# Gate products one product pair later, and three weight-sum stores one group later, in a gated SSM and MLP mixer

## The chip, the cores and the metric

The kernel runs on one core of a Trainium2 chip. The metric is the device time of one execution in microseconds (us). Three runs of the kernel before gave 563.6, 562.41 and 564.23 us; their median is 563.6 us.

## The reference

With x of 2048 tokens by 1024 features in bfloat16:

```python
g = sigmoid((x * gate_w).sum(-1))              # one gate per token
Bu = x @ B_bar.T                               # complex, 1024 states
h[t] = Lam_bar * h[t-1] + Bu[t]                # recurrence over 2048 tokens
a = 2 * Re(h @ C.T) + x * Dskip
b = gelu(layernorm(x) @ w1 + b1) @ w2 + b2     # F = 3584
out = g * a + (1 - g) * b
```

## The kernel before

**Products.** Nearly all matrix products are made by a scheme with seven products in place of eight: a 2 by 2 block product is cut into products p1 to p7 of blocks and of sums of blocks (class SG, L830 to L882; all of them go through `mm`, L813, whose first matmul stands on L822 or L824). The sums are made by VectorE through `dve_tt` (L885). The order on TensorE inside one group is p1, p7 of the group before, p5, p6, p2, p3, p4 of the group before.

**Stages on TensorE.** First x and B are transposed (L650, L666) and B's product with x is formed ("Bu"): `bu_plain(pt, c)` (L905) makes the plain product of state tile pt with token chunk c, one 8-matmul product each for the real and the imaginary part; it is used for pt 0 and 1 with chunks 0 and 1, and all else of Bu goes by `bu_group`. `z_gate(pr)` (L1027) makes the gate's sums over features for the two chunks of half pr: 16 matmuls with a two-column stationary matrix (L1036) into PSUM bank 7, then two evictions by ScalarE (L1043). Bank 7 is also one of the two banks (7 and 3) that the transposes of x and B go through; `t_b` (L657) evicts them on ScalarE (L670). Chunk 1 of x comes transposed by a DMA (L980).

Then comes the MLP: blocks "m" (x @ w1, seven groups each, `m_group`, L1254) and "b" (h @ w2, four groups, `b_group`) for two halves of F and two halves of the tokens, and at last the groups "y" (h @ C). The first block "m" is called here by its groups m0 to m6. The recurrence (`ssm`, L1123) is done by VectorE at a low priority between all this.

**W1.** Four slots (W1R, 7168 bytes per partition each) hold w1 column tiles and their sums. `w1_prep` (L1212) loads a tile (L1220), makes four sums in place (`dve_tt`), and, where the tile is wanted again in the second block, stores tile and sums to DRAM with a DMA from GpSimd's queue (L1235, 128 times 7168 bytes). The first four tiles are prepared ahead of the first block; of these the first three are stored, from slots 0, 1 and 2, and are loaded again (L1217) in the second block. The tile of m4 goes to slot 0, that of m5 to slot 1, that of m6 to slot 2: each load waits for the last product that reads the slot, and for the store from it. W2 comes in quarters (`w2_step`, L1285, load L1292, sums by `dve_tt`), one at the end of each of m0 to m3.

**Order.** `build` writes down a graph of tasks; `Graph.add` finds what each depends on, and a planner (`_schedule_once`, L225) simulates it with fixed costs and priorities and so fixes, before the run, the order of the instructions of every engine and queue. TensorE's order is fixed already: every product depends on the one before (`pe_last`). Each engine, and SyncE's and GpSimd's DMA queues, take their instructions in that order and wait at each. A change of the graph may change the planned order anywhere behind it on VectorE, ScalarE and both queues.

Of the kernel before, what the change touches and what calls it, by code (L numbers as in the profile page):

```python
# [419 lines left out]
def build(nc, A_x, A_Lambda_re, A_Lambda_im, A_B_re, A_B_im, A_C_re, A_C_im, A_log_dt, A_Dskip,  # L420
# [23 lines left out]
    g = Graph()  # L444
    es = ExitStack()
    with es:
# [73 lines left out]
        def ssem(name, k, final=False):  # L520
            key = (name, k)
            if key not in slot_sems:
                slot_sems[key] = sem("d_%s%d" % (name, k), dram=final)
                if final:
                    final_sems.append(slot_sems[key])
            return slot_sems[key]
# [378 lines left out]
        def bu_plain(pt, c):  # L905

            if c % 2 == 0:
                cev[pt, c // 2] = nxt("ev", NEV)
            ks = cev[pt, c // 2]
            for ri in range(2):  # L910
                bk = (4, 5, 6, 0, 1, 2)[nxt("cbank", 6)]
                ws = [AR.v(bqo(pt, 2 * ri) + dt * 256, [(1, 128)]) for dt in range(DT)]
                q = mm("bu%d.%d.%d" % (pt, c, ri), bk, ws, [xt(dt, c) for dt in range(DT)], True)
                ev = u_ev(pt, c // 2, ks, ri, c % 2)
                g.add("act", c_act(CH), (1.0, q), lambda e, ev=ev, bk=bk: e.activation(ev.ap, V(PS[bk], 0, [(1, 2 * T)]), AF.Copy),  # L915
                      reads=[b_ps[bk]], writes=[ev, b_ps[bk]], name="u%d.%d.%d" % (pt, c, ri))
                if c % 2 == 1:
                    u_store(pt, c // 2, ks, q, ri)
# [108 lines left out]
        def z_gate(pr):  # L1027

            cs = (2 * pr, 2 * pr + 1)
            xs = [[xt(dt, c) for c in cs] for dt in range(DT)]  # L1030

            def em(e):
                ins = None
                for dt in range(DT):
                    for i, c in enumerate(cs):
                        ins = e.matmul(bass.AP(PS[7], 32 * c * 512, [[512, 2], [1, CH]]), V(GWC, 2 * dt, [(1, 2)]), xs[dt][i].ap, start=(dt == 0), stop=(dt == DT - 1))  # L1036
                return ins
            seq[0] += 1
            t = g.add("pe", 1.0, (1.0, seq[0]), em, reads=xs + [b_gwc], writes=[b_ps[7]], name="z%d" % pr, extra=pe_last)
            pe_last[:] = [t]  # L1040
            for c in cs:
                o = bass.AP(AR.h[F32], 32 * c * zrow + ZR // 4, [[zrow, 2], [1, CH]])
                g.add("act", c_act(CH), (1.0, seq[0]), lambda e, c=c, o=o: e.activation(o, bass.AP(PS[7], 32 * c * 512, [[512, 2], [1, CH]]), AF.Copy),  # L1043
                      reads=[b_ps[7]], writes=[zr, b_ps[7]], name="ze%d" % c)
# [24 lines left out]
        for k in range(4, NTT):  # L1069
            load_x(k, (0.5, k))  # L1070
        for c in range(2):
            if c == 1:
                z_gate(0)
            for pt in range(2):
                bu_plain(pt, c)
        x_sums(0, seq[0])
        order = [(2, 0), (3, 0), (0, 1), (1, 1), (2, 1), (3, 1)] + [(pt, pr) for pt in range(4, PT) for pr in range(2)]
        summed = set()
# [133 lines left out]
        def w1_prep(j, first, q, o0, keep):  # L1212
            s = (o0 - W1R) // 7168
            w1slot[j] = o0
            if not first:
                o = AR.v(o0, [(1, 3584)])
                g.dma((10.0, q - 7), lambda e: e.dma_start(out=o.ap, in_=W1S[j]), 128 * 7168, ssem("w1", s), reads=[b_w1s[j]], writes=[o], name="w1l%d" % j)  # L1217
                return
            o = AR.v(o0, [(256, DT), (1, 256)])
            g.dma((10.0, q - 7), lambda e: e.dma_start(out=o.ap, in_=B_w1[:, j * 256:(j + 1) * 256].rearrange("(dt p) f -> p dt f", p=128)),  # L1220
                  D * 256 * 2, ssem("w1", s), writes=[o], name="w1_%d" % j, bw=DMA_BW_512)

            def raw(fo, dh, dt=BF16):
                return AR.v(o0 + (dh * 1024 + fo * 128) * 2, [(256, 4), (1, 128)], dt)

            def sq(i):
                return AR.v(o0 + 4096 + i * 1024, [(128, 4), (1, 128)], FP16)
            dve_tt("w1a%d" % j, q, sq(0), raw(1, 0), raw(1, 1), ALU.add, 512)
            dve_tt("w1b%d" % j, q, sq(1), sq(0), raw(0, 0), ALU.subtract, 512)
            dve_tt("w1c%d" % j, q, sq(2), raw(0, 0), raw(1, 0), ALU.subtract, 512)  # L1230
            dve_tt("w1d%d" % j, q, raw(1, 0, FP16), raw(0, 1), sq(1), ALU.subtract, 512)
            if not keep:
                return
            ov = AR.v(o0, [(1, 3584)])
            g.dma((10.0, q), lambda e: e.dma_start(out=W1S[j], in_=ov.ap), 128 * 7168, ssem("w1s", s, True), reads=[ov], writes=[b_w1s[j]], name="w1s%d" % j, q="pool")  # L1235

        def w1_st(j):
            o0 = w1slot[j]
# [265 lines left out]
        for n, it in enumerate(flat):  # L1504
            bi, x = it
            kind, Fh, c = blocks[bi]
            last_of_block = (n + 1 == len(flat)) or flat[n + 1][0] != bi
            nit = None if n + 1 == len(flat) else flat[n + 1]
            if (kind, Fh, c, x) == ("b", 1, 0, 3):
                y_load(0)  # L1510
                y_load(1)
            if (kind, x) == ("y", 0):
                y_load(2)
            if cur is None:
                cur = make(it)
                cur.p1()

            if prev is not None:
                prev.p7()
            if kind == "b" and x + 1 < 4:  # L1520
                prep_s((bi, x + 1), seq[0] + 4)
            if kind == "b" and Fh == 1 and c == 0 and x == 3:
                y_prep(0, seq[0] + 4)
            if kind == "y":
                if x + 1 < 8:
                    y_prep(x + 1, seq[0] + 4)
            if not early5:
                cur.p5()
            early5 = False
            cur.p6()  # L1530
            cur.p2()
            if nit is None:
                cur.p7()
            cur.p3()
            if prev is not None:
                prev.p4()
                if kind == "y" and 1 <= x and x + 2 < 8:
                    y_load(x + 2)
                if kind == "m":
                    w2_step(seq[0] + 19)  # L1540
                if kind == "m" and x > 0:
                    w1_next(18)
            if n == 0:
                def em_b2(e):
                    return [e.dma_start(out=v.ap, in_=bass.AP(B_b2.tensor, B_b2.offset + o, [[0, 128], [1, 512]])) for (v, o) in ((v_b2l, 0), (v_b2r, 512))]
                g.dma((40.0, 0), em_b2, 128 * 2048, sem("d_b2b"), writes=[v_b2l, v_b2r], name="b2b", ndma=2)
                g.add("dve", c_dve(512), (40.0, 1), lambda e: e.tensor_tensor(v_b2d.ap, v_b2r.ap, v_b2l.ap, ALU.subtract), reads=[v_b2l, v_b2r], writes=[v_b2d], name="b2d")
                for pg in range(PG):
                    for q in range(NQ):
                        ssm(pg, q)  # L1550
            prev, cur = cur, pend
            pend = None
            if last_of_block:
                if nit is None:
                    prev.p4()
                else:
                    nk = blocks[nit[0]][0]
                    if nk == "b":
                        prep = True
                        b0 = None  # L1560

                        cur = make(nit)
                        prev.p7()
                        cur.p1()
                        prev.p4()
                        w1_next(20)
                        prep_s(nit, seq[0])
                        pend = make((nit[0], nit[1] + 1))
                        pend.p1()
                    else:  # L1570
                        cur = make(nit)
                        prev.p7()
                        cur.p1()
                        cur.p5()
                        early5 = True
                        prev.p4()
                    prev = None
                if (kind, Fh, c) == ("m", 1, 0):
                    ct_load(seq[0] + 20)

                if kind == "m":
                    if (Fh, c) == (0, 0):
                        xn_load(1, seq[0] + 20)
                    elif (Fh, c) == (1, 1):
                        xn_load(0, seq[0] + 20)
                elif (Fh, c) == (0, 1):
                    w2_load(1)
# [43 lines left out]
```

## Time and profile before

| | |
|---|---|
| median of three runs | 563.6 us |
| the profiled execution | 563.84 us, its span 562.1 us |
| TensorE (PE) busy | 545.5 us, 97% of the span |
| VectorE (DVE) busy | 511.8 us, 91% |
| ScalarE (ACT) busy | 288.1 us, 51% |
| GpSimd (POOL) busy | 91.3 us, 16% |
| DMA | 120.08 MB, mean 214 GB/s |

A busy time is the time in which an engine had an instruction running. The chain that ended last goes through TensorE for 80% of the span and through VectorE for 14%. The times of the rows below count from the start of the span; a number in brackets at a row's end is how long the engine sat idle before it and what ended that. Behind a DMA the last number is the time from its issue until it had landed. The DMA share is the busy share of the 16 DMA engines; it can come out a little over 1.

### The profile page before, as it was taken

To read this page: it belongs to the slowest core of one execution; us is meant where nothing else is said; L and a number is where in the kernel's file an instruction comes from. 1 tells how busy PE (TensorE), PEld (TensorE's weight loads), DVE (VectorE), ACT (ScalarE), POOL (GpSimd) and SP (SyncE) were. 2 spreads that over 40 slices of the span, in tenths; PEclk is the share of its full clock that TensorE was granted. 3 is DMA by queue.
4 is the path that set the end of the run, shared out by engine and by line. 5 is a ranking of instruction groups with operands and counts; after the bars stand their busy time and mean duration, and the time that the engine had idled before them with its cause. 6 is when DMAs were issued, how large, how long until landed. Compare 5 with 4: busy or idle time off the path is not lost.

```text
span 562.1 us, 7384 instructions
## 1 busy us (share of the span) xinstructions
PE 545.5 (97%) x2553; PEld 249.2 (44%) x2601; DVE 511.8 (91%) x866; ACT 288.1 (51%) x481; POOL 91.3 (16%) x146
## 2 busy tenths in 40 slices
PE   5899999999999999999999999999999999999997
PEld 4444444444444444444444444444444444444443
DVE  3889899999999999999999999999999886978873
ACT  2978989667774247774246663236663322111110
POOL 0023757630000110011110000211000211001000
DMA  9994999989672444565456957688479999686621
GB/s 271 233 303 96 268 239 311 338 267 350 203 176 100 169 157 180 204 198 224 183 191 200 294 126 149 146 165 240 169 187 189 279 313 293 231 324 224 194 106 56
DMA packets 114911, 120.08 MB, mean 214 GB/s; under 512 B 70322, under 2 KB 92594, under 8 KB 113850
## 3 DMA queue, kind: packets, MB, share of 16 engines
q1 hardware_dynamic: 102256, 73.69, 47.0%
q0 software_dynamic: 12480, 45.90, 26.8%
q8 instruction: 20, 0.33, 0.2%
q14 instruction: 17, 0.14, 0.1%
q10 hardware_dynamic: 138, 0.02, 0.0%
HBM read 56.40 MB, written 47.46 MB: 185 GB/s over the span
## 4 chain that ended last, share of the span: by engine, by line
PE 80%; DVE 14%; issue 3%; ACT 2%; DMA 1%; SPq 0%; DVEq 0%; ACTq 0%
PE ps L824 59%; PE ps L822 19%; DVE ar L885 5%; DVE ar L1269 3%; DVE ar L1145 2%; DVE ar L1159 2%; DVE ar L1148 1%; DMA ar<-in_A_x_dram 1%; ACT ar L670 1%; PE ps L1036 1%; PE ps L650 0%; DVE ar L1352 0%; ACT ar L915 0%; ACT L714 0%; DVE ar L966 0%
## 5 line engine op out<-in xcount | busy, mean ns | idle before, releaser
L824 PE MATMUL ps<-ar 128*128 128x512 f16 (+1 forms) x1792 | 411.8, 379 | 4.7 <-DVE ar L1269 0.8
L824 PEld LDWEIGHTS ps<-ar 128*128 128x128 f16 (+1 forms) x1832 | 178.3, 98 | 221.0 <-ACT ps L857 2.8
L822 PE MATMUL ps<-ar 128*128 128x512 bf16 (+1 forms) x632 | 155.5, 379 | 1.3 <-DVE ar L885 0.9
L885 DVE TENSOR_TENSOR ar<-ar 128x512 f16<-128x512 bf16 (+6 forms) x216 | 139.1, 686 | 6.2 <-PE ps L822 1.8
L822 PEld LDWEIGHTS ps<-ar 128*128 128x128 bf16 (+1 forms) x640 | 61.9, 98 | 76.7 <-DVE ar L885 2.2
L1159 DVE TENSOR_TENSOR_SCAN ar<-cst,init,ar 128x256 bf16<-128x256 f32 x128 | 87.9, 735 | 0.4
L841 ACT ACTIVATE ar<-ps 128x512 f32<-128x512 f32 x100 | 59.0, 593 | 48.3 <-PE ps L822 37.8
L1145 DVE TENSOR_TENSOR ar<-ar 128x2048 bf16<-128x2048 bf16 x64 | 77.0, 1219 | 0.0
L857 ACT ACTIVATE ps<-ps 128x512 f32<-128x512 f32 x66 | 38.5, 583 | 69.9 <-PE ps L822 64.9
L1265 ACT ACTIVATE ar<-ps,cst 128x512 bf16<-128x512 f32 x56 | 38.4, 686 | 19.2 <-PE ps L824 18.5
L842 ACT ACTIVATE ar<-ps,cst 128x512 f32<-128x512 f32 x32 | 22.0, 688 | 49.2 <-PE ps L824 26.0
L1271 ACT ACTIVATE ar<-ar,cst 128x512 bf16<-128x512 f32 x56 | 40.1, 716 | 8.0 <-DVE ar L1269 7.7
L1349 ACT ACTIVATE ar<-ps,cst 128x512 f32<-128x512 f32 x32 | 22.0, 688 | 40.9 <-PE ps L824 40.6
L1148 DVE TENSOR_TENSOR ar<-ar 128x1024 bf16<-128x1024 bf16 x64 | 42.2, 686 | 0.1
L1269 DVE TENSOR_TENSOR ar<-ps,ar 128x512 f32<-128x512 f32 x56 | 38.4, 685 | 3.1 <-PE ps L824 2.5
L900 POOL DMA_DIRECT2D scr_u<-ar x32 | 25.1, 787 | 63.8 <-ACT ar L915 28.9
L1450 DVE SCALAR_TENSOR_TENSOR ar<-ps,cst,ar 128x512 bf16<-128x512 f32 x32 | 23.8, 749 | 12.1 <-PE ps L824 11.9
L1177 POOL DMA_DIRECT2D scr_h<-ar x16 | 9.6, 601 | 123.1 <-DVE ar L1148 123.1
L1352 DVE SCALAR_TENSOR_TENSOR ar<-ps,cst,ar 128x512 f32<-128x512 f32 x32 | 23.8, 744 | 4.4 <-PE ps L824 4.1
L1361 POOL DMA_DIRECT2D scr_ac<-ar x16 | 13.8, 879 | 83.5 <-DVE ar L1352 31.6
L1429 DVE SCALAR_TENSOR_TENSOR ar<-ar,cst 128x1024 f32<-128x1024 bf16 x16 | 20.4, 1282 | 0.2
L1359 POOL DMA_DIRECT2D scr_ac<-ar x16 | 8.5, 534 | 70.7 <-DVE ar L1352 41.0
(104 smaller groups left out, 244.2 us busy)
## 6 DMA issues: line engine op xcount, KB each, us to landing
scr_ac<-ar POOLq DMA_DIRECT2D x32, 512.0 KB, 5.0
ar<-in_A_x_dram SPq DMA_DIRECT2D x32, 256.0 KB, 5.2
scr_u<-ar POOLq DMA_DIRECT2D x32, 256.0 KB, 5.8
ar<-scr_u SPq DMA_DIRECT2D x16, 512.0 KB, 5.0
scr_h<-ar POOLq DMA_DIRECT2D x16, 512.0 KB, 5.8
ar<-scr_ac SPq DMA_DIRECT2D x16, 512.0 KB, 6.6
ar<-scr_h SPq DMA_DIRECT2D x8, 1024.0 KB, 7.3
ar<-in_B_w_dram SPq DMA_DIRECT2D x14, 512.0 KB, 6.8
```

Of the source, the lines that this page charges most:

```text
L822: ins = e.matmul(V(PS[bk], 0, [(1, n)]), st[i].ap, mv[i].ap, start=(i == 0), stop=(i == K - 1))
L824: ins = e.matmul(V(PS[bk], 0, [(1, n)]), st[i].ap, mv[i].ap, start=False, stop=(i == K - 1), skip_group_check=True)
L841: return e.activation(o.ap, V(PS[bk], 0, [(1, 512)]), AF.Copy)
L857: g.add("act", c_act(512), (pb[0], q - 2), lambda e: e.activation(V(PS[b], 0, [(1, 512)]), V(PS[a], 0, [(1, 512)]), AF.Copy), reads=[b_ps[ ...
L885: g.add("dve", c_tt16(n), (pb[0], q), lambda e: e.tensor_tensor(o.ap, a.ap, b.ap, op), reads=[a, b], writes=[o], name=nm).slack = slack
L900: g.dma((1.0, q), lambda e: e.dma_start(out=US[pt // 4, :, 4 * pr:4 * pr + 4, r0:r0 + T], in_=evv.ap), 2 * 128 * CH * 2, ssem("us", 2 * ks ...
L1145: g.add("dve", c_tt16(UE), pri(i), lambda e: e.tensor_tensor(o.ap, a.ap, tbl.ap, ALU.mult), reads=[a, tbl], writes=[o], name=nm + tag)
L1148: g.add("dve", c_tt16(UE // 2), pri(i), lambda e: e.tensor_tensor(o.ap, a.ap, b.ap, op), reads=[a, b], writes=[o], name=nm + tag)
L1159: lambda e, pt=pt, ri=ri, vin=vin, go=go: e.tensor_tensor_scan(go.ap, Cb("R", pt, T), vin.ap, V(INIT, pt * 2 + ri, [(1, 1)]), ALU.mult, AL ...
L1265: g.add("act", c_act(512, ap_operands=1), (10.0, q + 1), lambda e: e.activation(o.ap, V(PS[bk], 0, [(1, 512)]), AF.Gelu_apprx_tanh, bias=C ...
L1269: g.add("dve", c_dve(512), (10.0, q - 2), lambda e: e.tensor_tensor(sv.ap, V(PS[bk], 0, [(1, 512)]), sv.ap, ALU.add), reads=[b_ps[bk], sv] ...
L1271: g.add("act", c_act(512, psum=False, ap_operands=1), (10.0, q + 3), lambda e: e.activation(o.ap, sv.ap, AF.Gelu_apprx_tanh, bias=C("B1", ...
```

## The change

Two things. `z_gate(0)` is called after `bu_plain(0, 1)` instead of before it. And the stores of w1 tiles that are prepared ahead of the first block (those made while no product has been put down since the end of Bu) are not put down at once: their numbers are kept in a list, and the stores are put down at the start of the second round of the loop over groups (n == 1), with a dependence on the last product put down by then, which is p4 of the last Bu group, at the end of m0's products.

```diff
         for c in range(2):
-            if c == 1:
-                z_gate(0)
             for pt in range(2):
                 bu_plain(pt, c)
+                if (c, pt) == (1, 0):
+                    z_gate(0)
         x_sums(0, seq[0])
...
             if not keep:
                 return
+            if seq[0] == bu_seq[0]:
+                w1_held.append(j)
+            else:
+                w1_store(j)
+
+        w1_held = []
+        bu_seq = [seq[0]]
+
+        def w1_store(j, extra=()):
+            o0 = w1slot[j]
+            q = seq[0]
             ov = AR.v(o0, [(1, 3584)])
-            g.dma((10.0, q), lambda e: e.dma_start(out=W1S[j], in_=ov.ap), 128 * 7168, ssem("w1s", s, True), reads=[ov], writes=[b_w1s[j]], name="w1s%d" % j, q="pool")
+            g.dma((10.0, q), lambda e: e.dma_start(out=W1S[j], in_=ov.ap), 128 * 7168, ssem("w1s", (o0 - W1R) // 7168, True), reads=[ov], writes=[b_w1s[j]], name="w1s%d" % j, q="pool", extra=extra)
...
                 y_load(2)
+            if n == 1:
+                for j in w1_held:
+                    w1_store(j, pe_last)
             if cur is None:
                 cur = make(it)
                 cur.p1()
```

## Rows read from the trace of the kernel before

**Rows 1.** The page, engines: busy us, share of the span, instructions.
```profile
PE 545.5 (97%) x2553; PEld 249.2 (44%) x2601; DVE 511.8 (91%) x866; ACT 288.1 (51%) x481; POOL 91.3 (16%) x146
```
**Rows 2.** Waits of PE from 23 us on: total us, times, longest.
```profile
PE ps L1036 <- DVE ar L762: 1.4, 1, 1.4
PE ps L822 <- DVE ar L885: 0.9, 1, 0.9
PE ps L824 <- DVE ar L1269: 0.8, 1, 0.8
...
PE ps L824 <- DVE ar L1352: 0.2, 1, 0.2
```
**Rows 3.** Timeline of PE, 19 to 36 us: start, us, instruction.
```profile
21.25 0.61 PE L666 MATMUL ps<-ident,ar 128*128 128x128 bf16 x8
23.28 1.89 PE L1036 MATMUL ps<-ar,gwc 128*2 128x512 bf16 x16 [1.43 <-DVE ar L762]
25.11 8.81 PE L822 MATMUL ps<-ar 128*128 128x512 bf16 x39
```
**Rows 4.** Timeline of ACT, 20 to 24 us.
```profile
21.60 0.63 ACT L915 ACTIVATE ar<-ps 128x512 bf16<-128x512 f32 x1
22.07 1.06 ACT L670 ACTIVATE ar<-ps 128x1024 bf16<-128x1024 bf16 x1
```
**Rows 5.** SP's queue and DMA issues from 6.8 us: chunk 1 of x.
```profile
6.83 7.25 SPq L980 DMA_TRANSPOSE ar<-in_A_x_dram  x1
...
ar<-in_A_x_dram SPq DMA_TRANSPOSE x1, 9.7
```
**Rows 6.** Stretches: PE, PEld, DVE, ACT, POOL busy us; PEclk, DMA share, GB/s.
```profile
76.00:125.00 49.00, 48.19 (x221) 21.60 (x223) 48.83 (x91) 37.38 (x69) 28.48 (x40) 1.00 1.02 291
125.00:149.00 24.00, 23.66 (x109) 10.45 (x110) 23.90 (x38) 17.44 (x30) 1.30 (x2) 1.00 1.03 344
126.00:148.00 22.00, 21.66 (x99) 9.54 (x100) 21.90 (x36) 16.13 (x27) 1.30 (x2) 1.00 1.04 347
150.00:156.00 6.00, 6.00 (x29) 2.66 (x28) 6.00 (x11) 4.84 (x9) 0.00 (x0) 1.00 0.01 4
102.00:104.00 2.00, 2.00 (x11) 0.88 (x9) 2.00 (x6) 1.60 (x4) 1.93 (x3) 1.00 1.03 414
```
**Rows 7.** Timeline of POOL, 90 to 135 us: the three stores.
```profile
94.32 0.63 POOL L1235 DMA_DIRECT2D scr_w<-ar  x1 [0.15 <-DVE ar L971]
...
107.19 0.62 POOL L1235 DMA_DIRECT2D scr_w<-ar  x1 [0.29 <-DVE ar L885]
...
124.41 0.55 POOL L1235 DMA_DIRECT2D scr_w<-ar  x1 [1.05 <-DVE ar L885]
```
**Rows 8.** Line 1235, all six stores: issue ns, and landing.
```profile
L1235 POOL DMA_DIRECT2D scr_w<-ar x6: 534/543/628, 94.3 to 257.2; - x6
...
DMA to landing us min/median/max: 4.1/5.3/8.8
```
**Rows 9.** Timeline of PE: end of Bu, m4, and the wait at 166 us.
```profile
122.99 1.04 PE L824 MATMUL ps<-ar 128*128 128x512 f16 x4 [0.43 <-ACT ar L969]
...
142.44 1.03 PE L822 MATMUL ps<-ar 128*128 128x512 bf16 x4
...
166.08 6.22 PE L824 MATMUL ps<-ar 128*128 128x512 f16 x27 [0.54 <-DVE ar L885]
```
**Rows 10.** Timeline of SP's queue, 120 to 152 us: W2 and m4's W1.
```profile
124.09 0.37 SPq L1292 DMA_DIRECT2D ar<-in_B_w_dram  x1
...
130.16 0.38 SPq L1292 DMA_DIRECT2D ar<-in_B_w_dram  x1
130.67 0.76 SPq L1220 DMA_DIRECT2D ar<-in_B_w_dram  x1
```
**Rows 11.** DMA issues at 130.6 to 130.9 us: KB, us to landing.
```profile
ar<-in_B_w_dram SPq DMA_DIRECT2D x1, 512.0 KB, 10.2
```
**Rows 12.** DMA queues, 127 to 131 us: packets, MB, share of 16 engines.
```profile
q1 hardware_dynamic: 634, 0.65, 52.7%
q0 software_dynamic: 126, 0.82, 49.6%
```
**Rows 13.** Timeline of DVE: W2's first sum, W1's sums for m4.
```profile
140.74 2.00 DVE L885 TENSOR_TENSOR ar<-ar 128x3584 f16<-128x3584 bf16 x1
...
143.26 1.55 DVE L885 TENSOR_TENSOR ar<-ar 128x512 f16<-128x512 bf16 x4
```

## The prediction

> **What bounds the kernel now.** I read four things in this order. First the page's engine line [rows 1]: TensorE is busy 97% of the span, so time can only be won where it stands idle, or lost by making it idle. Then TensorE's waits from 23 us on [rows 2]: the largest single one, 1.43 us, stands in front of the gate products of the first half, and all others together are small; the 0.5 us before a product at 166 us and the 0.43 us at 123 us [rows 9] belong to them. Third, the stretches [rows 6]: from 76 to 149 us VectorE is busy in all but 0.3 us, and the DMA engines are busy without a break, with a granted TensorE clock of 1.00 (2.4 GHz) in every stretch. From 150 to 156 us DMA share is 0.01. So in the stretch where the MLP begins, three resources are full at once, and TensorE stays fed with little to spare. Last, I looked at what is queued on GpSimd's and SyncE's queues there [rows 7, 10].
>
> One execution's numbers make the sum: 563.84 us, which is 0.24 us over the median of 563.6 us. About 0.3% (1.69 us) is what a measurement can tell from no change: faster means below 561.91 us, slower above 565.29 us.
>
> **Part 1, the gate products.** The gate products wait although chunk 1 of x has long come: its DMA was issued at 6.83 us and landed 9.7 us later, at 16.5 us [rows 5]. The row names VectorE as releaser, but the instruction it names finished next to it by chance; the gate products need bank 7, and the last transpose of B in that bank is evicted by ScalarE from 22.07 to 23.13 us [rows 4], 0.15 us before they start at 23.28 us [rows 3]. ScalarE could not begin sooner, since it was evicting a product before. The transposes on TensorE end at 21.86 us [rows 3]. After the change the product pair of chunk 1 stands here; it needs chunk 1 (there), the first B tile and two banks that no one has used yet. So it starts at about 21.9 us. The pair is 16 of the 39 matmuls of 8.81 us [rows 3], 3.6 us, so the gate products come at about 25.5 us, when bank 7 has been free for 2 us. The 16 gate matmuls and their two evictions cost the same as before; no DMA is issued by the moved step itself. The evictions of the pair now come ahead of the gate's on ScalarE and the first store of u follows them about 3.5 us earlier on GpSimd's queue, which has nothing ahead of it. Gain: 1.43 us, from 25 us on.
>
> Is it kept? VectorE hardly idles after 76 us, so TensorE would run into VectorE where it started later than now; but VectorE's work is set off by TensorE's results and by DMAs that TensorE's progress releases, so I let the whole machine move 1.43 us earlier. Bounds: nothing kept (VectorE does not move), or 1.43 plus the two gaps of 0.43 and 0.54 us [rows 9], 2.4 us. I take 1.43.
>
> **Part 2, the stores.** What is removed: two of the three stores leave 94 to 112 us (issues at 94.32 and 107.19 us [rows 7]). TensorE waits for no DMA there [rows 2], so this wins nothing on TensorE; the third store, at 124.41 us, stays where it was. What is added: all three are now released by the last product of Bu, whose four matmuls begin at 122.99 us and last 1.04 us [rows 9], so at about 124.0 us on the old time axis. GpSimd's queue issues them one behind the other, 0.63 us each at most [rows 8]; behind them waits one store of u, which no engine needs soon.
>
> The DMA engines do mind. Two stores are 2 x 896 KB, 1.84 MB, put into a stretch that is already full from 126 to 148 us at 347 GB/s [rows 6]. At that rate they take 5.3 us; at 414 GB/s, which the stretch from 102 to 104 us shows [rows 6], 4.4 us. A queue that has nothing to do with them is slowed too: while the one store of before ran, from 127 to 131 us, GpSimd's queue q0 had 49.6% of the engines and SyncE's q1 52.7% [rows 12]. Now the same sharing lasts three times as long, and q1 carries what the MLP needs next: W2's first two quarters (issued at 124.09 and 130.16 us) and the W1 tile for m4 (130.67 us) [rows 10].
>
> The W1 tile is the one with least slack. It landed 10.2 us after its issue [rows 11], at 140.9 us; m4's first product starts at 142.44 us [rows 9]. Slack: 1.57 us. Bounds of its delay: nothing, if the stores' bytes fit in beside; 5.3 us, if all go ahead of it at 347 GB/s. I take 4.4 us, nearer to the upper end, because the stretch has no idle share to give [rows 6] and the stores enter the queue 6 us ahead of the tile. TensorE then waits 4.4 - 1.57 = 2.8 us before m4. VectorE's sums of that tile, at 143.26 us [rows 13], are held by the same landing, not by a second one. m5's and m6's tiles come under the same delay, but then m4's wait has moved their products too. W2's sum at 140.74 us [rows 13] shares the delay; while VectorE stands there, the recurrence waits, not TensorE. Part of the 2.8 us comes back: the 0.54 us at 166 us [rows 9] is VectorE being late, and TensorE's wait gives VectorE time to catch up.
>
> Sum: 563.84 - 1.43 + 2.8 - 0.54 = 564.67 us; 0.24 us less on the scale of the median: **564.4 us**.
>
> GpSimd's issue of such a store took 534 to 628 ns in all six cases [rows 8], also while VectorE was never idle [rows 6]; so I charge no wait for it. The Trainium skill's page "SBUF — State Buffer", section "SBUF: two separate sides", says that GpSimd cannot write a DMA's descriptors while VectorE runs certain fast two-port instructions. By that rule each of three issues in a row could stand behind a VectorE instruction, and the sum would be the 566.4 us of the fourth rival; by the rows it is 564.4 us, and this trace does not show the rule at work.
>
> **The rivals.**
>
> *The stores are hidden.* The tile is delayed by less than its slack of 1.57 us, because what the stores push aside is traffic that nobody waits for. For it: the DMA engines idle from 150 us on [rows 6], so the pile can drain. Against it: the tile's transfer lies inside the full stretch. Time: 563.6 - 1.43 = 562.2 us, and 561.6 if the gap of 0.54 us goes as well. Chance 0.32.
>
> *The gaps go as well.* Without two stores the stretch from 94 to 124 us has less traffic, sums come earlier, and a new plan has none of the waits of 0.43, 0.5 and 0.9 us [rows 2, 9]: 563.6 - 1.43 - 1.8 = 560.4 us, or 561.2 with half of them. Chance 0.10.
>
> *Slower: the tile's issue is late too.* Its slot 0 must first be emptied by the store, which now starts 30 us later. Release at 124.0 us and landing after 4.1, 5.3 or 8.8 us [rows 8] gives 128 to 132.8 us; the tile was issued at 130.67 us. From a landing of more than 6.6 us on, SyncE's queue stands at this load and everything behind it. At 8.8 us the tile is 2.2 us later on top of the 4.4: TensorE waits 5.0 us, 563.6 - 1.43 + 5.0 = 567.2 us; halfway, 566.1 us. The change as a whole is slower than before once the tile comes 3.0 us late (1.57 + 1.43). Against it: the 8.8 us were those of a store that shared the engines with two loads, and here the first of three stores goes first. Chance 0.11.
>
> *GpSimd held up by VectorE.* If the first store's issue stood behind VectorE's longest instruction, 2.00 us [rows 13], the slot would come free that much later: 564.4 + 2.0 = 566.4 us. [...] Rows 8 speak against it. Chance 0.02.
>
> *No effect of the move.* ScalarE, or a changed plan, puts the 1.43 us back at a later wait, and the stores are hidden: 563.6 us. Chance 0.03.
>
> **How the numbers follow.** The forecast has the remaining chance, 0.42. Its own range is 563.0 (a delay of 3.0 us, slack and gain just paid) to 565.6 us (5.3 us, nothing regained); a third of it lies above 565.29 us. Faster: 0.14 of the hidden stores' 0.32 (those that also close a gap or shift the plan favourably) and all of the 0.10: 0.24. Slower: 0.14 from the forecast, 0.10 of the late issue, 0.02 of GpSimd: 0.26. The same: the rest, 0.50. The range reaches down to 561.3 us, between the second rival's two values, and up to 566.4 us; what is left out is half of that rival and half of the late issue, and some room for a plan that differs elsewhere.
>
> **What the profile after would show.** Part 1 is right if no idle time stands before the gate products, and the product pair starts near 21.9 us. Part 2 is right if three rows of line 1235 stand together at about 122.6 us, DMA share stays full until 152 us or later, and the first product of m4 has an idle time of 2 to 3 us ended by a DMA of W1. I am wrong if that product starts without a wait: then the stores were hidden. I am also wrong if new waits for VectorE stand far from either place; then the plan moved, which no row here can price.

## The result, and the profile after

The changed kernel takes a median of 567.18 us (17 runs) against 563.73 us for the kernel before in the same comparison: ratio 1.0062, 95% interval 1.0047 to 1.0078, 3.45 us longer. The forecast was 564.4 us, 0.8 us above before. The profiled execution is one of the longer ones, 570.06 us with a span of 568.3 us, so its rows are compared with the 563.84 us of the profile before.

TensorE's waits from 23 us on (us in total, times, longest), the kernel after:

```profile
PE ps L824 <- ACT ps L857: 3.3, 3, 2.1
PE ps L822 <- DMA ar<-in_B_w_dram: 2.4, 1, 2.4
PE ps L824 <- ACT ar L841: 1.6, 2, 0.9
PE ps L822 <- DVE ar L885: 1.5, 2, 1.1
PE ps L824 <- DVE ar L1280: 0.3, 1, 0.3
PE ps L824 <- DVE ar L885: 0.3, 1, 0.3
```

They add up to 9.4 us; all seven rows of this view before [rows 2] add up to 4.6 us. The wait for line 1036 is gone, the wait for a DMA of W1 or W2 is new, and the largest row names ScalarE's line 857 (a copy from PSUM to PSUM with which a product group is seeded). The timeline of TensorE shows where they stand:

```profile
20.73 0.61 PE L666 MATMUL ps<-ident,ar 128*128 128x128 bf16 x8
21.17 3.62 PE L822 MATMUL ps<-ar 128*128 128x512 bf16 x16
24.72 1.89 PE L1036 MATMUL ps<-ar,gwc 128*2 128x512 bf16 x16
26.54 5.35 PE L822 MATMUL ps<-ar 128*128 128x512 bf16 x24
...
71.46 3.63 PE L824 MATMUL ps<-ar 128*128 128x512 f16 x16 [2.12 <-ACT ps L857]
...
84.14 3.63 PE L824 MATMUL ps<-ar 128*128 128x512 f16 x16 [0.42 <-ACT ps L857]
...
91.15 2.12 PE L824 MATMUL ps<-ar 128*128 128x512 f16 x9 [0.79 <-ACT ps L857]
...
147.80 1.60 PE L822 MATMUL ps<-ar 128*128 128x512 bf16 x4 [2.44 <-DMA ar<-in_B_w_dram]
149.20 1.91 PE L824 MATMUL ps<-ar 128*128 128x512 f16 x4
152.23 1.04 PE L822 MATMUL ps<-ar 128*128 128x512 f16 x4 [1.12 <-DVE ar L885]
```

The gate products follow the product pair without a wait, where before 1.43 us stood ahead of them [rows 3]. The product at 147.80 us is m4's first one: it waits 2.44 us for its W1 tile, as forecast in kind and place. The product pair starts 0.7 us sooner than forecast; 0.5 us of that is this execution's own, since its transposes end at 21.34 us (20.73 + 0.61) and not at 21.86 us. The waits at 71, 84 and 91 us stand nowhere in the prediction. The two rows of four matmuls at 147.80 and 149.20 us are long. The stretches (columns as in [rows 6]) show the granted clock there:

```profile
60.00:76.00 16.00, 13.88 (x65) 6.03 (x63) 10.66 (x19) 11.98 (x24) 9.48 (x16) 1.00 1.12 225
66.00:68.00 2.00, 2.00 (x11) 0.91 (x10) 0.00 (x0) 0.60 (x1) 0.00 (x0) 1.00 0.74 55
68.00:70.00 2.00, 1.34 (x7) 0.39 (x4) 0.06 (x1) 0.07 (x1) 0.00 (x0) 1.00 1.18 75
...
149.00:150.00 1.00, 1.00 (x3) 0.30 (x2) 0.93 (x2) 0.56 (x2) 0.00 (x0) 0.50 1.15 298
...
156.00:160.00 4.00, 4.00 (x20) 1.77 (x19) 4.00 (x6) 2.44 (x5) 0.00 (x0) 1.00 0.07 22
```

Behind the wait the clock is at its lower level (0.50, 1.2 GHz). The eight matmuls take from 147.80 to 151.11 us, 3.3 us; at the full clock they take 1.9 us (142.99 to 144.89 us in the trace of the run with the early order of before, below). That is 1.4 us. Waits and clock come to 9.4 - 4.6 + 1.4 = 6.2 us, and 570.06 - 563.84 is 6.22 us. That the two agree so well is in part chance: the rows start at 23 us and do not hold the 0.5 us by which the transposes ended sooner, so about 0.5 us of the later loss stands in no row.

The three stores stand where the change puts them, the first one released by TensorE (GpSimd's timeline):

```profile
126.13 0.55 POOL L1246 DMA_DIRECT2D scr_w<-ar  x1 [1.68 <-PE ps L824]
...
127.56 1.09 POOL L1246 DMA_DIRECT2D scr_w<-ar  x2
```

The DMA engines stay full until 156 us (before: until about 149 us [rows 6]). And from 66 to 70 us they move only 55 to 75 GB/s, while VectorE does next to nothing. VectorE's timeline there:

```profile
63.25 1.46 DVE L1011 TENSOR_SCALAR ar<-ar,cst 128x1024 bf16<-128x1024 bf16 x3
69.94 0.69 DVE L971 TENSOR_TENSOR ar<-ar 128x512 bf16<-128x512 f32 x1 [5.22 <-DMA scr_u<-ar]
```

It stands 5.22 us for a store of u, whose buffer it must overwrite; that store was issued at 58.19 us and landed 11.7 us later. ScalarE waits for the same store, with the seed (line 857) behind it, which explains the row at 71 us:

```profile
69.92 0.60 ACT L960 ACTIVATE ar<-ps 128x512 bf16<-128x512 f32 x1 [3.33 <-DMA scr_u<-ar]
...
70.82 0.59 ACT L857 ACTIVATE ps<-ps 128x512 f32<-128x512 f32 x1
```

In the trace before, VectorE's longest wait between 60 and 76 us is 0.9 us. Nothing in the diff touches that place. What moved is the plan: on VectorE, ScalarE and both queues the order of the instructions differs from early on. SyncE's queue, for example, now has a transpose of B's imaginary part ahead of the three loads of u for the recurrence instead of behind them.

### The profile page after: what moved, and what is told of

It reads as the page before. It is cut to its first block, busy times and chain, and to the rows that moved or that the text cites. A ratio compares the mean times of both kernels' runs of the same rounds, so it can differ in the third digit from the quotient of the medians.

```text
span 568.3 us, 7422 instructions
## 1 busy us (share of the span) xinstructions
PE 550.1 (97%) x2601; PEld 249.2 (44%) x2601; DVE 511.6 (90%) x866; ACT 287.3 (51%) x481; POOL 93.4 (16%) x146
## 4 chain that ended last, share of the span: by engine, by line
PE 81%; DVE 9%; DMA 5%; ACT 2%; issue 2%; POOL 1%; SPq 0%; ACTq 0%; DVEq 0%
PE ps L824 59%; PE ps L822 20%; DVE ar L885 3%; DMA ar<-in_B_w_dram 2%; DMA scr_u<-ar 2%; DVE ar L1159 1%; DVE ar L1145 1%; DVE ar L1280 1%; PE ps L666 1%; PE ps L650 1%; DMA ar<-in_A_x_dram 1%; PE ps L1036 1%; DVE ar L1011 1%; ACT ar L991 0%; DVE ar L1148 0%
## 5 line engine op out<-in xcount | busy, mean ns | idle before, releaser
L822 PE MATMUL ps<-ar 128*128 128x512 bf16 (+1 forms) x640 | 157.8, 380 | 3.9 <-DMA ar<-in_B_w_dram 2.4
L1372 POOL DMA_DIRECT2D scr_ac<-ar x16 | 13.7, 858 | 83.6 <-DVE ar L1363 31.1
L960 ACT ACTIVATE ar<-ps 128x512 bf16<-128x512 f32 x28 | 16.8, 599 | 7.4 <-PE ps L824 3.8
```

Of the source, the lines that this page charges most:

```text
L822: ins = e.matmul(V(PS[bk], 0, [(1, n)]), st[i].ap, mv[i].ap, start=(i == 0), stop=(i == K - 1))
```

## The experiments

All differences below are to the kernel before in the same comparison. To tell the change apart from the plan that it sets off, some kernels take the order of VectorE, ScalarE and both queues from a list (PIN) in place of the planner's (TensorE's is fixed already):

```diff
         g.schedule(horizon=HORIZON)
+        for pe_, names_ in PIN.items():
...
+            g.order[pe_] = pinned
```

**Each part alone, with a plan of its own.** Gate move without held stores (first diff, against the kernel before), held stores without gate move (second, against the changed kernel):

```diff
-            if c == 1:
-                z_gate(0)
             for pt in range(2):
                 bu_plain(pt, c)
+                if (c, pt) == (1, 0):
+                    z_gate(0)
```

```diff
+            if c == 1:
+                z_gate(0)
             for pt in range(2):
                 bu_plain(pt, c)
-                if (c, pt) == (1, 0):
-                    z_gate(0)
```

> The gate products moved, the stores not held; the planner orders the queues anew. Theory A (two separate causes: the new plan that the gate move brings costs some 4 us of TensorE's waits between 70 and 100 us; the held stores cost 2.4 us and more before m4): 563.7 - 1.4 + 4.0 = 566.3 us, waits at 70 to 100 us as in the changed kernel, none before m4. Theory C (the held stores are to blame for all): 562.3 us and none of these waits. Theory B (TensorE being 1.4 us earlier collides with the DMAs, whatever the plan): 566.3 us as well.

> The stores held, the gate products where they were before; the planner orders the queues anew. Theory A: no wait at 70 to 100 us, a wait of 2 to 3 us before m4 ended by the DMA of its W1 tile, and the granted clock at half for some us behind it: 566 to 568 us. Theory C: all waits of the changed kernel, 568 us or more. If the held stores were hidden: 563.7 us.

Gate move alone: 580.02 us, ratio 1.0301 (1.0275 to 1.0327), far outside of what any theory said. TensorE's timeline of that run:

```profile
130.18 3.60 PE L824 MATMUL ps<-ar 128*128 128x512 bf16 x8 [15.18 <-ACT ar L841]
```

In the stretches 100 to 108 us little was moved:

```profile
100.00:104.00 4.00, 4.00 (x20) 1.81 (x19) 4.00 (x8) 3.97 (x9) 2.56 (x5) 1.00 1.25 117
104.00:108.00 4.00, 4.00 (x19) 1.82 (x19) 3.93 (x6) 2.70 (x5) 3.51 (x4) 1.00 1.09 112
```

and its DMA issues from 96 to 104 us what was in flight (KB, us to landing):

```profile
scr_w<-ar POOLq DMA_DIRECT2D x2, 896.0 KB, 18.1
...
ar<-in_B_w_dram SPq DMA_DIRECT2D x1, 512.0 KB, 23.0
...
ar<-scr_xn SPq DMA_TRANSPOSE x2, 12.0
```

The new plan issued the first two stores at 97.43 and 99.53 us, when the DMA transposes of the normalized x were running; before, one stood at 94.32 us and the next at 107.19 us [rows 7]. The DMA share was over 1, and 112 to 117 GB/s were moved. VectorE stood 6.5 us for a load of W1 and 4.9 us for a transpose between 100 and 135 us, ScalarE stood for VectorE, and TensorE for ScalarE.

Held stores alone: 566.41 us, 1.0053 (1.0035 to 1.0072), with a wait of 2.79 us before m4, ended by a DMA of W1, at a granted clock of 1.00. So a wait before m4 comes from the held stores without any gate move.

**The same edits with the order of before.** In the lists below names are instructions in their planned order. Third kernel: only the gate's two evictions (ze) moved in ScalarE's list; fourth: the two held stores (w1s) moved in GpSimd's list as well, ahead of the third one:

```diff
-ln_sq1 ze0 ze1 u0.1.0 ln_sq2 u0.1.1
+ln_sq1 u0.1.0 ln_sq2 u0.1.1 ze0 ze1
...
-ln_nmr2 w1s0 us5.1.0
+ln_nmr2 us5.1.0
...
-ln_nmr3 w1s1 us6.1.0
+ln_nmr3 us6.1.0
...
-us7.0.1 w1s4
+us7.0.1 w1s0 w1s1 w1s4
```

> The gate products moved, with VectorE, ScalarE, GpSimd and SyncE in the order of the kernel before (only the gate's two evictions behind the pair's on ScalarE). Theory A: the 1.43 us are kept and nothing is given back: 562.3 us, no waits at 70 to 100 us over 0.5 us. Theory B: the waits at 70 to 100 us are there as well, about 566 us.

> The whole change, with all queues in the order of the kernel before (the two stores moved behind the release, ahead of the third). Theory A: 562.3 us and the cost of the held stores alone, 2.4 to 5 us: 564.7 to 567.3 us, with the wait before m4 and none at 70 to 100 us. Theory B: as the changed kernel, 567 us, with both stretches of waits.

Gate move: 561.4 us, ratio 0.9965 (0.9929 to 1.0000), no gap at the gate products. Both: 565.97 us, 1.0036 (1.0020 to 1.0052); TensorE waits 1.90 us for VectorE, which waited 3.32 us for a DMA of b2, and 0.70 us for W1 right behind. The gate move with the order of before was run once more below, and once with a store moved as well; the three agree on 1.5 to 2.3 us less than before. The first part was priced right, as long as nothing else moves.

**Bytes, or the slot?** To the gate move with the order of before, extra stores of 896 KB are added at the place of the held ones, from a table to an array that nobody reads; no slot waits for them:

```diff
+            if n == 1:
+                for j in range(2):
...
+                    g.dma((10.0, seq[0]), lambda e, j=j, xv=xv: e.dma_start(out=XTRA[j], in_=xv.ap), 128 * 7168, ssem("w1x", j, True), reads=[xv], writes=[B("xtra%d" % j)], name="xtra%d" % j, q="pool", extra=pe_last)
```

> Gate move, the order of before on all queues, the three stores where they were; only added: two stores of 896 KB each (from the rotation tables to a scratch array that nobody reads) on GpSimd's queue behind the end of Bu, where the held stores would be. No slot waits for them. Bytes theory: they alone delay the W1 tile of m4, so TensorE waits 1.5 to 3 us before m4, and the time is 564 to 566 us against 561.4 us without them. Slot theory (it is slot 0's late release by its own store that delays the tile's issue): no wait before m4 over 0.7 us, time 561 to 562.3 us.

> As the kernel with two extra stores of 896 KB, but with one. Bytes theory: each extra store delays m4's W1 tile by its own transfer, about 2.2 us, so one exceeds the tile's slack of 1.57 us by about 0.6 us: wait before m4 0 to 1 us, time 562 to 564 us, about halfway between 561.8 (no extra store) and 565.0 us (two). Rival (the queue with three stores in a row is a threshold of its own): one store costs nothing, no wait before m4, time 561.2 to 562.2 us.

Two extra stores: 565.03 us, ratio 1.0025 (1.0005 to 1.0044). m4's first product in TensorE's timeline:

```profile
144.46 1.04 PE L823 MATMUL ps<-ar 128*128 128x512 bf16 x4 [2.12 <-DMA ar<-in_B_w_dram]
```

and its W1 tile in the DMA issues at 129.1 us:

```profile
ar<-in_B_w_dram SPq DMA_DIRECT2D x1, 512.0 KB, 15.3
```

One extra store: 562.77 us, 0.9984 (0.9970 to 0.9998), no wait before m4, and the tile (issued at 129.52 us) in

```profile
ar<-in_B_w_dram SPq DMA_DIRECT2D x1, 512.0 KB, 11.8
```

Without extra stores it took 10.1 us from an issue at 129.10 us. So one store delays the tile by 1.7 us, about its slack of 1.57 us, and two by 5.2 us: bytes alone do it. They do not do it evenly, the second store cost twice what the first one did; but the profile with two stores is of that kernel's longest execution (567.58 us). In the changed kernel slot 0 is not late either: the tile is issued at 133.58 us, 11.8 us ahead of where m4 would begin without its wait (147.80 - 2.44 us); before it was 142.44 - 130.67 = 11.8 us as well [rows 9, 10].

**Is the rest chance, or one place?** The changed kernel once more; the new order without held stores, its first two stores 10 us later, clear of the transposes; the gate move with the order of before once more; and the same with its first store clear of the transposes. The last of these differs from the third kernel by

```diff
-ln_nmr2 w1s0 us5.1.0
+ln_nmr2 us5.1.0
...
-ln_nmr3 w1s1 us6.1.0
+ln_nmr3 w1s0 w1s1 us6.1.0
```

and the second has w1s0 and w1s1 behind us5.1.1 (a store of u) in the new order.

> The changed kernel once more, unaltered, for a second profile of it. Theory: the wait of about 2.4 us before m4 is the held stores' doing and comes again (1.9 to 3 us, ended by a DMA); the 2.1 us wait near 71 us, behind an 11.7 us landing of a store of u, is not: the kernel with the gate move alone has the same order up to there and showed no wait of more than 0.4 us at that place, so here it should be under 1 us, and the time 565 to 568 us. Rival: the wait near 71 us belongs to the new order and comes again with 2 us; then it is a term of its own, and the time is 567 us or more.

> Gate move, the new planned order everywhere, and the stores not held, but the first two of them put on GpSimd's queue about 10 us later, at about 111 us, behind the DMA transposes of the normalized x. Theory: what cost the gate move alone 16 us was two stores of 896 KB that run beside these transposes; apart from each other the transposes land within 11 us of their issue, no wait over 1.5 us is left on TensorE, none over 1 us before m4, and the time is 561.5 to 564 us. Rival (the new order itself is slower, whatever the stores do): 567 us or more, with waits for VectorE between 70 and 170 us.

> Gate move alone with the order of before, once more for a narrower interval. Theory (the 1.43 us is kept, and some of the gaps behind it close): 561.0 to 562.3 us, ratio 0.995 to 0.998. Rival (the first measurement was a lucky one and VectorE gives nothing back): 563 to 564 us.

> Gate move alone with the order of before, and the first store of a W1 tile put 13 us later on GpSimd's queue, behind the DMA transposes of the normalized x, directly ahead of the second store. Theory: this store, running beside the transposes, brings the stretch from 92 to 96 us down to 110 to 150 GB/s and sometimes makes TensorE wait (3.76 us at 99 us in one profile); apart, no such dip is left between 88 and 98 us, no wait over 0.5 us between 90 and 130 us, and the time is 560.5 to 561.8 us with no execution over 564 us. Rival: the dip belongs to the transposes alone: then it is there again, and the time is 561.4 to 562.2 us.

The second look at the changed kernel, a single execution, took 570.47 us and shows the wait near 71 us again (1.77 us), with 2.81 us before m4: the rival was right, the wait is the new order's. With the stores moved 10 us, the 15 us wait was gone, but 566.07 us, 1.0039 (1.0019 to 1.0059), is above what the theory allowed: its order costs without any held store. Its profile is of its shortest execution (563.28 us). Even there VectorE stands 1.4 us for a store of u between 55 and 76 us, and TensorE waits, from 23 us on,

```profile
PE ps L822 <- DVE ar L885: 2.3, 2, 2.0
PE ps L824 <- ACT ar L841: 2.2, 2, 1.5
PE ps L824 <- DVE ar L1269: 0.3, 1, 0.3
PE ps L824 <- DVE ar L885: 0.3, 1, 0.3
```

The 2.0 us, at 145 us, are a wait for VectorE's sums inside m4, with no store held. The gate move with the order of before gave 562.03 us, 0.9963 (0.9938 to 0.9987). Its profiled execution was its longest, 566.62 us, with this wait:

```profile
99.07 2.98 PE L824 MATMUL ps<-ar 128*128 128x512 bf16 x8 [3.76 <-ACT ar L841]
```

In that execution VectorE stood 5.0 us for a W1 load until 94 us. So such a loss can happen with the order of before too; of its 21 executions two took over 566 us. With the store apart: 561.56 us, 0.9959 (0.9944 to 0.9973), none of 12 runs over 561.95 us: by its ratio the **fastest version**, though not clear of the gate move alone. Half of that theory failed: the stretch from 92 to 94 us still moved only 89 GB/s, so that store is not what slows the transposes there.

**Single instructions of the new order.** The changed kernel with the loads of u put back ahead of the transpose on SyncE's queue; then, besides, the seeds on ScalarE put ahead of two table activations (tab) and of a scaling (e2t) that waits for VectorE:

```diff
-bTd6.0 bTd5.1 ul0.0 ul0.1 ul0.2
+bTd6.0 ul0.0 ul0.1 ul0.2 bTd5.1
...
-su_u4.1 tab_c4 u4.2.0 tab_s4 seed_u5.0
+su_u4.1 u4.2.0 seed_u5.0 tab_c4 tab_s4
...
-u4.2.1 e2t0_6 seed_u5.1 uc5.1.1
+u4.2.1 seed_u5.1 uc5.1.1 e2t0_6
```

> The changed kernel with its new order everywhere, but one instruction put back on SyncE's queue: the three first loads of u for the recurrence come ahead of the second transpose of B's imaginary part of tile 5 again, as before the change. Theory: the wait of 1.8 to 2.1 us near 71 us, in both profiles of the changed kernel, is the new queue order's doing (the loads land at 69 to 70 us behind a transpose, VectorE stands, and TensorE behind it); put back, it falls under 0.8 us, the wait of 2.4 to 2.8 us before m4 stays, and the time is 564.5 to 566.5 us. Rival: the wait near 71 us comes from DMA transposes that run into stores, whatever their order; then it comes again in some executions and the time stays 566.5 to 568 us.

> As the kernel with the loads of u put back, and on ScalarE two copies into PSUM that TensorE waits for (near 83 and 90 us) are put ahead of what the new order set before them: two table activations of 1.05 us each, and one scaling that waits for VectorE. Theory: the new order's own cost sits in such places; the waits of 0.97 and 0.80 us at 83.5 and 90.5 us fall under 0.3 us each, what is saved is kept, and the time is 566.0 to 566.9 us against 567.7 us. Rival: VectorE is the bound there and behind; the two waits vanish but come back as longer ones before 160 us, and the time stays 567.3 to 568.0 us.

Neither helped: 567.7 us, 1.0072 (1.0054 to 1.0091), and 567.76 us, 1.0078 (1.0056 to 1.0101). In the first the wait at 71 us is gone, but VectorE now stands for another DMA in the same stretch (its waits from 55 to 76 us):

```profile
DVE ar L885 <- DMA ar<-in_A_B_im_dram: 3.7, 1, 3.7
```

In the second the waits for line 857 are gone, and TensorE's waits for line 841 (ScalarE's evictions, behind VectorE) grew from 1.5 to

```profile
PE ps L824 <- ACT ar L841: 3.7, 5, 1.0
```

So its rival holds as far as these profiles go: what VectorE lost before 76 us comes out as waits of TensorE somewhere before 131 us, wherever ScalarE's queue lets it.

**The early or the late part of the new order?** The whole change with the order of before up to about 94 us and the new order from there on; and the reverse, without held stores.

> The whole change, but every engine and queue keeps the order of before up to about 94 us and takes the new order from there on. Theory: the loss that belongs to the new order arises between 60 and 76 us, where VectorE stands 4 to 5 us for a DMA, and TensorE pays for it until 131 us. Then VectorE stands under 2.5 us there, TensorE's waits between 60 and 130 us come to under 1.2 us (4.0 in the changed kernel's profile), only the wait before m4 and the one behind it are left, and the time is 564.5 to 566.2 us. Rival (the loss sits in the later part of the new order): VectorE stands as little, but the time stays 566.6 us or more.

> The counterpart: gate move alone, no store held (the first one behind the transposes, as in the kernel with that store apart), the new order up to about 94 us and the order of before from there on. Theory: VectorE stands 3 us or more for a DMA between 60 and 76 us in most executions, TensorE's waits between 60 and 130 us come to 2 us or more, and the time is 563.3 to 566 us against 561.6 us with the early order of before. Rival: the early part of the new order costs nothing; 561.2 to 562.3 us.

The whole change with the early order of before: 564.01 us, 1.0018 (0.9996 to 1.0040), 1.07 us above before: a difference that is not clear of noise, and less than the theory allowed. VectorE waits for no DMA between 55 and 76 us, TensorE not at all between 23 and 140 us. m4's start in its timeline:

```profile
142.99 1.04 PE L822 MATMUL ps<-ar 128*128 128x512 bf16 x4 [3.09 <-DMA ar<-in_B_w_dram]
143.86 1.03 PE L824 MATMUL ps<-ar 128*128 128x512 f16 x4
146.10 1.04 PE L822 MATMUL ps<-ar 128*128 128x512 f16 x4 [1.22 <-DVE ar L885]
```

What is left, in its waits from 23 us on, is

```profile
PE ps L822 <- DMA ar<-in_B_w_dram: 3.1, 1, 3.1
PE ps L822 <- DVE ar L885: 1.6, 2, 1.2
PE ps L824 <- DVE ar L885: 0.5, 2, 0.3
PE ps L824 <- DVE ar L1280: 0.4, 1, 0.4
```

The reverse: 565.42 us, 1.0038 (1.0014 to 1.0062), 2.5 us above before where the same without the new early order is 1.9 us below it. VectorE's waits from 55 to 76 us:

```profile
DVE ar L971 <- DMA scr_u<-ar: 3.0, 1, 3.0
```

TensorE waits at 82, 89, 97, 103 and 125 us, 3.9 us in all, each time for ScalarE. The early part of the new order is what the prediction lacked: 2.4 us with held stores (3.45 - 1.07), 4.4 us without (2.5 + 1.9). In both pairs the intervals lie apart.

The way from before to the changed kernel can be walked in three steps: -1.9 us for the gate move (store apart), +2.9 us for the held stores (1.07 + 1.88, late order new), +2.4 us for the early order. That they end at the measured 3.45 us proves nothing, since each is a difference between neighbours. And the prices depend on the way: with no store held the early order costs 4.4 us, and the held stores add 0.9 us (3.45 - 2.57, not clear of noise) to a kernel that has the whole new order already. The two losses overlap.

## Why the prediction was wrong

*The step that failed* is the one behind Part 1: "VectorE's work is set off by TensorE's results and by DMAs that TensorE's progress releases, so I let the whole machine move 1.43 us earlier." Its bounds ran from nothing kept to 2.4 us gained and held no loss. The machine did not move, it was re-planned: VectorE came to stand 1.4 to 5.2 us for DMAs between 60 and 76 us in every profile with the new early order, and at most 0.9 us in those with the order of before. From 76 us on it has 0.3 us of idle time in 73 us [rows 6], so it can't catch up, and TensorE paid: the swap of the early order alone is worth 2.4 to 4.4 us. The rival that named a changed plan gave back the 1.43 us at most and had a chance of 0.03. The prediction's last sentence, that new waits for VectorE far from either place would mean that the plan moved, came true in kind (the waits at 71, 84 and 91 us name ScalarE, which stood for the same store as VectorE at 70 us); the price of that was left out of the range. (The top of the forecast's own range was also added up wrong: 563.6 - 1.43 + 5.3 - 1.57 is 565.9 us, not 565.6 us. The measured 567.18 us lies above either.)

*Part 1 itself was right.* No gap at the gate products, the pair at 21.2 us in the changed kernel, and 1.5 to 2.3 us gained with the order of before; 1.43 us was taken.

*Part 2 was right in kind, and in the wait before m4 nearly in size.* The tile's delay was taken as 4.4 us and measured 4.0 us (14.2 against 10.2 us [rows 11]); the wait as 2.8 us and measured 2.44 us, and 2.79 and 3.09 us where the held stores came without the gate move or with the early order of before. Slot 0's late release, the one rival here, fell with the tile's issue at 133.58 us; that the stores are hidden, the other, fell with these waits.

*Two terms of Part 2 came out otherwise, both by the new order.* I wrote that VectorE's sums are "held by the same landing, not by a second one": a second wait of 1.1 to 1.2 us for these sums follows in the changed kernel and in the run with the early order of before. It is not the held stores' doing: it stands there with 2.0 us in the new order without held stores, and in none of the kernels with the late order of before (at most 0.3 us).

And 0.54 us were to come back at 166 us because TensorE's wait gives VectorE time to catch up. The whole change with the order of before is the test of this. TensorE waits 1.90 and 0.70 us ahead of m4 there, and yet 0.5 us at 166 us and 0.9 + 0.9 us around 335 us are left:

```profile
PE ps L824 <- DVE ar L1280: 2.8, 2, 1.9
PE ps L822 <- DVE ar L885: 0.9, 1, 0.9
PE ps L822 <- DMA ar<-in_B_w_dram: 0.7, 1, 0.7
PE ps L824 <- DVE ar L885: 0.5, 1, 0.5
```

In the new late order 0.2 us come back at 166 us (0.32 us left in the run with the early order of before), and the waits around 335 us shrink from 1.7 us (0.8 + 0.9 [rows 2]) to 0.7 us, in the kernel without held stores as well. So what came back came from the plan, and that 564.01 us for the whole change with the early order of before lies so near to the forecast is luck: in the order of before throughout the change took 565.97 us, 2.3 us over before, where 0.8 us was forecast.

*GpSimd held up by VectorE* was rightly small: the six stores took 532 to 550 ns to issue (line 1246), against 534 to 628 ns before [rows 8].

What stays open is which instruction of the early order makes VectorE stand. Putting back one place on SyncE's queue changed the DMA it stands for, not the time. The wait also differs between executions and kernels: 5.2 and 4.9 us in the two profiles of the changed kernel, 3.0 us in that of the new early order with the late one of before, 1.4 us in that of the new order without held stores. That VectorE's wait is what TensorE pays for is read from the profiles, in which both come and go together; no run made VectorE wait and changed nothing else.

## What to carry to other kernels

Where a planner fixes the order, an edit has two prices, its own and that of the new plan; measure the edit once with the old order, and before forecasting put a loss in the range for each engine that has no idle time to catch up with. Do not add up prices that were measured under different plans. A transfer that is moved into a full stretch delays the next one by its bytes, and costs only what exceeds that one's slack: here one store of 896 KB caused no wait before m4, the second one of 2 us. What is gained at one engine is kept only if a full engine behind it, here VectorE, isn't made to wait for a DMA on the way.

## What the hardware showed that I had not expected

While DMA transposes are in flight there are stretches in which the DMA share stays high and little is moved: 55 to 75 GB/s from 66 to 70 us in the changed kernel (share 0.74 to 1.18), 112 to 117 GB/s for 8 us in the gate move alone, where a W1 load of 512 KB took 23.0 us (10.2 us for one of the same size in [rows 11]). The kernel before has shorter ones: 102 GB/s from 66 to 68 us, 110 GB/s from 94 to 96 us. Moving two stores by 10 us took the wait of 15 us away, but stores are not needed for such a stretch: in the dip at 92 to 94 us of the kernel with the store apart GpSimd's queue moved nothing, and SyncE's 0.18 MB. Which transfer slows which was not isolated. The Trainium skill's page "DMA: Bandwidth & Descriptors", section "Latency and other measured facts", gives 261 GB/s for a DMA transpose with a non-contiguous middle dimension and 350 to 400 GB/s for a contiguous one. These stretches lie far below both, but they are short and hold other transfers too; no run here measures a transpose by itself.

TensorE's granted clock fell to 0.50 (1.2 GHz) for about 3 us right behind an idle time of 2.44 us in the changed kernel, but stayed at 1.00 behind 3.09 and 1.22 us of idle time in the run with the early order of before, and behind 2.79 us with the held stores alone. It was 0.50 from 146 to 149 us in the profile with two extra stores, behind a wait of only 2.12 us. The changed kernel itself differs from execution to execution: in eight of its 17 the mean granted clock was 0.990 to 0.997, and their median is 568.85 us; in nine it was 0.999 or 1.000, with a median of 566.72 us. I can't tell from these rows what decides; a wait of this size can cost 1.4 us more than its length, or not.
